# Pooled attention and a top-1 mixture of experts on one core: one PSUM ring, a shifted attention stream, a later gate chain, a reordered start and a column-split last block

## Chip, cores, metric

The kernel runs on one core of one Trainium2 chip (trn2). The metric is the device time of one execution in microseconds (us), as the median of repeated runs. Every profile below is of one execution.

## What is computed

Eight batches, eight heads, 576 tokens, head size 64. Keys and values are averaged over groups of 8 tokens, so each head has 72 keys. The attention output (4608 tokens of 512) goes through a cosine router that takes one of eight experts per token; the experts are two layers, 512 to 1024 to 512.

```python
k_p = k.reshape(B, H, Sp, pool, D).mean(axis=3)
v_p = v.reshape(B, H, Sp, pool, D).mean(axis=3)
attn = softmax(scale * np.matmul(q, k_p.transpose(0, 1, 3, 2)))
x = np.matmul(attn, v_p)            # then tokens x 512
logits = (x / |x|) @ (emb / |emb|).T / tau
expert_idx = np.argmax(logits, axis=1)
gate_w = softmax(logits)[expert_idx]
out[mask] = gate_w[mask] * (np.maximum(x[mask] @ w1[e], 0.0) @ w2[e])
```

## The kernel before

For each batch the kernel picks the expert that most of its tokens choose, loads that expert's weights and runs its FFN over all 576 tokens; tokens that chose another expert are put right in a loop at the end, which runs zero times when there are none.

`attn_steps(b)` lists the attention of a batch: pooling of k and v (`_pool`, L179: matmuls with a 0/1 matrix `pmat`, two 64-row halves in turn), transposes of q (`qtr`, L200, L206) and of pooled k (`_kpt`), eight score heads (L241) each with an exponential on ScalarE (L248), five chunks of 128 tokens of PV (L265) with the division on VectorE (reciprocal `r` L272, scaling `x_sb` L274), their transposes into `xt_all` (L285, L290), routing (L312) and the choice (`_expert`, L330 to L384). `_expert` counts tokens per expert, GpSimd reads the index and starts the two weight loads (L89, L92). Then comes the gate chain: GpSimd takes a power (`ssq`, L355), VectorE scales the logits (L357 to L364), ScalarE takes their exponential (L367), VectorE makes the gate `gm` (L369 to L378).

`ffn_steps` lists an FFN: 16 groups of the first layer (`hgrp`, 4 matmuls of 288 columns, L406), evicted in turn by ScalarE (L411) and VectorE (L413) into `hT`; then five blocks of output rows (`yblk`, 8 matmuls of 512 columns, L423), the fifth with 64 rows, scaled by the gate on VectorE (L434) or ScalarE (L431) and stored by the sync queue (SP).

Attention of batches 0 and 1 runs alone; then `merge` interleaves FFN b with the attention of b + 2, in proportion to a cost noted beside each step. FFN 6 and 7 run alone. The order written is the order on each engine. PSUM has 8 banks: two 2-bank tiles `pa` for attention and four 1-bank tiles `pf` for the FFN. GpSimd's queue carries the loads of k, v, q and the weights; each costs it time to write descriptors.

Of the kernel before, what the change touches and what calls it, by code (L numbers as in the profile page):

```python
# [2 lines left out]

# [9 lines left out]
I32 = mybir.dt.int32  # L13

# [12 lines left out]
def kernel(  # L27
# [25 lines left out]

    const = ctx.enter_context(tc.tile_pool(name="const", bufs=1))
# [12 lines left out]
    def psa():  # L67
        return ps_a.tile([128, 1024], FP32, name="pa")

    def psf():  # L70
        return ps_f.tile([128, 512], FP32, name="pf")


    def load_qkv(b):
        kv = inp.tile([128, 2, HP, T * D], FP16, name="kv")
        qq = inp.tile([128, HP, T * D], FP16, name="qq")

        def view(a):
            return a[b].rearrange("(hp h2) (p t) d -> (h2 p) hp (t d)", h2=2, t=T)

        nc.gpsimd.dma_start(out=kv[:, 0], in_=view(k))
        nc.gpsimd.dma_start(out=kv[:, 1], in_=view(v))
        nc.gpsimd.dma_start(out=qq, in_=view(q))
        return kv, qq
# [13 lines left out]
    loads = {0: load_qkv(0)}  # L98


    ident_h = const.tile([128, 128], FP16)
    make_identity(nc, ident_h)
    ident_f = const.tile([128, 128], FP32)
    make_identity(nc, ident_f)
    loads[1] = load_qkv(1)

    pmat = const.tile([128, T, G], FP16)
    nc.vector.memset(pmat, 1.0)
    for half in range(2):
        sl = pmat[ts(half, 64)]  # L110
        nc.gpsimd.affine_select(out=sl, in_=sl, pattern=[[1, T], [-POOL, G]],
                                compare_op=ALU.is_ge, fill=0.0, base=0,
                                channel_multiplier=T)
        nc.gpsimd.affine_select(out=sl, in_=sl, pattern=[[-1, T], [POOL, G]],
                                compare_op=ALU.is_ge, fill=0.0, base=POOL - 1,
                                channel_multiplier=-T)
    ones_m = const.tile([128, 128], FP16)
    nc.vector.memset(ones_m, 1.0)
    iota8 = const.tile([128, E], FP32)
    nc.gpsimd.iota(iota8, pattern=[[1, E]], base=0, channel_multiplier=0,  # L120
                   allow_small_or_imprecise_dtypes=True)
    tie = const.tile([128, E], FP32)
    nc.vector.tensor_scalar(out=tie, in0=iota8, scalar1=-1e-7 * XS, scalar2=None,
                            op0=ALU.mult)
    tie_n = const.tile([128, E], FP32)
    nc.vector.tensor_scalar(out=tie_n, in0=iota8, scalar1=-0.001, scalar2=None,
                            op0=ALU.mult)
    half_c = const.tile([128, NC], FP32)
    nc.vector.memset(half_c, 0.5)
    pair_b = const.tile([1, B * E], I32)  # L130
    nc.gpsimd.iota(pair_b, pattern=[[1, B], [0, E]], base=0, channel_multiplier=0)
    pair_e = const.tile([1, B * E], I32)
    nc.gpsimd.iota(pair_e, pattern=[[0, B], [1, E]], base=0, channel_multiplier=0)

    enT = const.tile([128, 4, E], FP16)
    emb = const.tile([E, DM], FP32)
    nc.sync.dma_start(out=emb, in_=moe_expert_emb)
    emb_sq = const.tile([E, DM], FP32)
    emb_n = const.tile([E, 1], FP32)
    nc.scalar.activation(out=emb_sq, in_=emb, func=AF.Square, accum_out=emb_n)  # L140
    nc.gpsimd.tensor_tensor(out=emb_n, in0=emb_n, in1=half_c[:E, 0:1], op=ALU.pow)
    nc.vector.tensor_scalar(out=emb_n, in0=emb_n, scalar1=1e-6, scalar2=tau,
                            op0=ALU.add, op1=ALU.mult)
    nc.vector.reciprocal(out=emb_n, in_=emb_n)
    nc.vector.tensor_scalar_mul(out=emb, in0=emb, scalar1=emb_n)
    ent_ps = psa()
    for w in range(4):
        nc.tensor.transpose(out=ent_ps[:, ts(w, E)], in_=emb[:, ts(w, 128)],
                            identity=ident_f[:E, :E])
    nc.vector.tensor_copy(out=enT, in_=ent_ps[:, 0:4 * E].rearrange("p (w e) -> p w e", e=E))  # L150
# [5 lines left out]
    ext_f = keep.tile([1, B, E], FP32)  # L156

    weights = {}
    gates = {}


    def attn_steps(b):
# [9 lines left out]
        @step(2.0)  # L172
        def _pool():
            kv, _ = loads[b]
            pk = psa()
            for t in range(T):
                for par in range(2):
                    rows = ts(par, 64)
                    nc.tensor.matmul(  # L179
                        out=pk[0:G, ts(par, 512)],  # L180
                        lhsT=pmat[rows, t, :],
                        rhs=kv[rows, :, :, ts(t, D)].rearrange("p a h d -> p (a h) d"),
                        start=(t == 0), stop=(t == T - 1))
# [68 lines left out]
        for h in range(H):  # L252
            step(0.2)(lambda h=h: score(h))

        st['ssq'] = None

        def pv(c):
            if c == 0:
                st['ssq'] = rt.tile([128, NC], FP32, name="ssq")
                nc.vector.memset(st['ssq'], 1.0)  # L260
                st['xs'] = {}
            L = 128 if c < 4 else 64
            px = psa()
            for h in range(H):
                nc.tensor.matmul(  # L265
                    out=px[0:L, h * 128:h * 128 + D + 1],
                    lhsT=st['at', h][:, c * 128:c * 128 + L],
                    rhs=st['vpx'][:, h // 2, h % 2, :],
                    start=True, stop=True)
            pxv = px[0:L].rearrange("p (h c) -> p h c", c=128)  # L270
            r = xp.tile([128, H], FP32, name="r")
            nc.vector.reciprocal(out=r[0:L], in_=pxv[:, :, D])  # L272
            x_sb = xp.tile([128, H, D], FP16, name="x_sb")
            nc.vector.tensor_tensor(  # L274
                out=x_sb[0:L], in0=pxv[:, :, 0:D],
                in1=r[0:L].unsqueeze(2).to_broadcast([L, H, D]), op=ALU.mult)
            st['xs'][c] = x_sb

        def xtr(c):
# [3 lines left out]
            pt = psa().bitcast(FP16)  # L283
# [7 lines left out]
            else:  # L291
# [3 lines left out]
            sq = xp.tile([128, H * D], FP16, name="sq")  # L295
            nc.scalar.activation(out=sq[0:L], in_=xf[0:L], func=AF.Square,  # L296
                                 accum_out=st['ssq'][0:L, c:c + 1])

        order = [('p', 0), ('p', 1), ('x', 0), ('p', 2), ('x', 1), ('p', 3),
                 ('x', 2), ('p', 4), ('x', 3), ('x', 4)]  # L300
        for kind, c in order:
            if kind == 'p':
                step(0.5)(lambda c=c: pv(c))
            else:
                step(0.3)(lambda c=c: xtr(c))

        @step(1.0)
        def _route():
            pl = psa()
            for c in range(NC):  # L310
                for w in range(4):
                    nc.tensor.matmul(out=pl[:, ts(c, E)],  # L312
                                     lhsT=xt_all[:, b, w, ts(c, 128)], rhs=enT[:, w, :],
                                     start=(w == 0), stop=(w == 3))
            lg = rt.tile([128, NC, E], FP32, name="lg")
            nc.vector.tensor_tensor(
                out=lg, in0=pl[:, 0:NC * E].rearrange("p (c e) -> p c e", e=E),
                in1=tie.unsqueeze(1).to_broadcast([128, NC, E]), op=ALU.add)
            lmax = rt.tile([128, NC], FP32, name="lmax")
            nc.vector.tensor_reduce(out=lmax, in_=lg, axis=AX.X, op=ALU.max)  # L320
            oh = oh_all[:, b]
            nc.vector.tensor_tensor(out=oh, in0=lg,
                                    in1=lmax.unsqueeze(2).to_broadcast([128, NC, E]),
                                    op=ALU.is_ge)
# [70 lines left out]
    def ffn_steps(xt, get_w, get_gm, finish):  # L395
# [166 lines left out]
```

## Time and profile before

| | us |
|---|---|
| median of 3 runs (lowest, highest) | 313.42 (313.03, 313.93) |
| the profiled execution, its own time | 315.35 |
| its span, first to last instruction | 313.8 |
| TensorE busy in it | 245.4 |

PE is TensorE's matmuls, PEld its weight loads, DVE VectorE, ACT ScalarE, POOL GpSimd, SP the sync engine. A row of a timeline gives the start, the busy time and, in brackets, how long the engine had been idle and what released it. The granted clock is a share of 2.4 GHz (0.50 is 1.2 GHz). Line numbers are those of the kernel before; the changed kernel has its own.

### The profile page before, as it was taken

How to read it: one execution, taken by the hardware profiler on the slowest of the kernel's cores; microseconds unless marked ns; L12 is line 12 of the kernel's file. 1: busy time of each engine (PE TensorE's matmuls, PEld its weight loads, DVE VectorE, ACT ScalarE, POOL GpSimd, SP SyncE). 2: the span in 40 equal slices, each digit the busy share in tenths (PEclk: the TensorE clock that was granted, in tenths of full speed). 3: DMA queues.
4: the chain of work that ended last, by engine and by line, in shares of the span. 5: the costliest groups of instructions: out<-in, count | busy, mean ns of one | idle time of the engine just before them, and what ended most of it. 6: DMA issues, size and time to landing. Idle time of an engine off the chain costs nothing.

```text
span 313.8 us, 5182 instructions
## 1 busy us (share of the span) xinstructions
PE 245.4 (78%) x1980; PEld 141.0 (45%) x1981; DVE 144.7 (46%) x445; ACT 108.2 (34%) x252; POOL 45.1 (14%) x65
## 2 busy tenths in 40 slices
PE   0376737689995999869995989599995999299990
PEld 0234423446453644545453645264553545164740
DVE  1135552745563637363664455363835456332410
ACT  2036117325431273126422344037412642121410
POOL 8400050060006000140006000410012000300000
PEclk9985565589998699979999899969997999789998
DMA  6980099669945994299747994399539414784142
GB/s 104 207 142 2 0 169 209 120 106 210 210 104 93 209 207 95 63 190 208 146 102 121 210 192 104 62 206 207 117 77 179 90 37 104 123 157 111 41 99 58
DMA packets 26924, 40.75 MB, mean 130 GB/s; under 512 B 1800, under 2 KB 14088, under 8 KB 26896
## 3 DMA queue, kind: packets, MB, share of 16 engines
q0 software_dynamic: 21120, 30.94, 56.3%
q1 hardware_dynamic: 5776, 9.46, 12.9%
q8 instruction: 16, 0.26, 0.3%
q14 instruction: 12, 0.10, 0.1%
HBM read 61.88 MB, written 9.44 MB: 227 GB/s over the span
## 4 chain that ended last, share of the span: by engine, by line
PE 60%; DVE 14%; ACT 9%; POOL 8%; issue 5%; POOLq 1%; DVEq 0%; ACTq 0%
PE pf L423 20%; PE pf L406 19%; ACT at L248 6%; DVE x_sb L274 4%; PE pa L265 4%; PE pa L241 4%; PE pa L206 3%; PE pa L179 3%; POOL ssq L355 3%; DVE y_sb L434 2%; PE pa L312 2%; POOL w L92 2%; PE pa L285 2%; DVE kpT L224 1%; ACT hT L411 1%
## 5 line engine op out<-in xcount | busy, mean ns | idle before, releaser
L406 PE MATMUL pf<-xt_all,w 128*128 128x288 f16 x512 | 84.5, 313 | 25.7 <-ACT hT L411 25.7
L423 PE MATMUL pf<-w,hT 128*128 128x512 f16 (+1 forms) x320 | 78.7, 380 | 0.0
L406 PEld LDWEIGHTS <-w 128*128 128x128 f16 x512 | 50.4, 106 | 48.6 <-issue 31.1
L248 ACT ACTIVATE at<-pa 72x576 f16<-72x576 f32 x64 | 38.4, 646 | 16.7 <-PE pa L241 16.6
L413 DVE TENSOR_SCALAR hT<-pf 128x288 f16<-128x288 f32 x64 | 27.9, 450 | 29.2 <-PE pf L406 29.0
L423 PEld LDWEIGHTS <-hT 128*128 128x128 f16 (+1 forms) x320 | 28.3, 100 | 25.8 <-issue 0.8
L411 ACT ACTIVATE hT<-pf 128x288 f16<-128x288 f32 x64 | 25.6, 408 | 41.0 <-PE pf L406 41.0
L89 POOL DMA_DIRECT2D w<-in_moe_w_dram x8 | 6.1, 760 | 224.2 <-PE pf L406 117.5
L296 ACT ACTIVATE sq<-x_sb 128x512 f16<-128x512 f16 (+1 forms) x40 | 24.9, 625 | 20.0 <-DVE x_sb L274 19.8
L274 DVE TENSOR_TENSOR x_sb<-pa,r 128x512 f16<-128x512 f32 (+1 forms) x40 | 27.6, 690 | 2.8 <-ACT sq L296 0.5
L434 DVE TENSOR_SCALAR y_sb<-pf,gm 128x512 f32<-128x512 f32 (+1 forms) x24 | 17.9, 746 | 20.7 <-PE pf L423 20.7
L265 PE MATMUL pa<-vpx,at 72*128 72x65 f16 (+1 forms) x320 | 20.2, 208 | 8.3 <-DVE x_sb L274 5.4
L241 PE MATMUL pa<-qT,kpT 64*72 64x256 f16 (+1 forms) x128 | 21.7, 332 | 5.4 <-ACT at L248 2.9
L367 ACT ACTIVATE lg<-lg 128x40 f32<-128x40 f32 x8 | 1.9, 236 | 68.0 <-DVE lg L364 68.0
L431 ACT ACTIVATE y_sb<-pf,gm 128x512 f32<-128x512 f32 x16 | 11.0, 687 | 36.1 <-PE pf L423 36.1
L265 PEld LDWEIGHTS <-at 72*128 72x128 f16 (+1 forms) x320 | 15.6, 108 | 17.2 <-DVE x_sb L274 9.1
L272 DVE RECIPROCAL r<-pa 128x8 f32<-128x8 f32 (+1 forms) x40 | 8.1, 203 | 30.7 <-PE pa L265 30.7
L179 PE MATMUL pa<-kv,pmat 64*72 64x512 f16 x144 | 22.1, 462 | 0.0
L206 PE MATMUL pa<-ident_h,qq 128*128 128x128 f16 x128 | 15.5, 257 | 5.0 <-DVE vpx L190 5.0
L285 PE MATMUL pa<-ident_h,x_sb 128*128 128x128 f16 (+1 forms) x160 | 16.7, 234 | 2.3 <-DVE x_sb L274 2.3
L207 DVE COPY qT<-pa 128x1152 f16<-128x1152 f16 x16 | 12.1, 756 | 12.7 <-PE pa L206 12.5
L241 PEld LDWEIGHTS <-kpT 64*72 64x72 f16 x128 | 7.9, 113 | 21.4 <-issue 16.4
(82 smaller groups left out, 178.2 us busy)
## 6 DMA issues: line engine op xcount, KB each, us to landing
w<-in_moe_w_dram POOLq DMA_DIRECT2D x16, 1024.0 KB, 10.0
out_dram<-y_sb SPq DMA_DIRECT2D x72, 128.0 KB, 2.4
kv<-in_k_dram POOLq DMA_DIRECT2D x8, 576.0 KB, 13.8
kv<-in_v_dram POOLq DMA_DIRECT2D x8, 576.0 KB, 15.9
qq<-in_q_dram POOLq DMA_DIRECT2D x8, 576.0 KB, 18.0
emb<-in_moe_expert_emb_dram SPq DMA_DIRECT2D x1, 16.0 KB
```

Of the source, the lines that this page charges most:

```text
L179: nc.tensor.matmul(out=pk[0:G, ts(par, 512)], lhsT=pmat[rows, t, :], rhs=kv[rows, :, :, ts(t, D)].rearrange("p a h d -> p (a h) d"), start ...
L206: nc.tensor.transpose(out=pq[:, ts(blk, 128)], in_=src, identity=ident_h)
L241: nc.tensor.matmul(out=pS[0:G, c0:c0 + nb * 64].rearrange("g (t p) -> g t p", p=64), lhsT=st['kpT'][rows, h if j == 0 else h ^ 1, :], rhs= ...
L248: nc.scalar.activation(out=at, in_=pS[0:G, c0:c0 + S], func=AF.Exp, scale=escale)
L265: nc.tensor.matmul(out=px[0:L, h * 128:h * 128 + D + 1], lhsT=st['at', h][:, c * 128:c * 128 + L], rhs=st['vpx'][:, h // 2, h % 2, :], sta ...
L274: nc.vector.tensor_tensor(out=x_sb[0:L], in0=pxv[:, :, 0:D], in1=r[0:L].unsqueeze(2).to_broadcast([L, H, D]), op=ALU.mult)
L296: nc.scalar.activation(out=sq[0:L], in_=xf[0:L], func=AF.Square, accum_out=st['ssq'][0:L, c:c + 1])
L406: nc.tensor.matmul(out=ph[:, 0:HALF], lhsT=w1v[:, kk, w // 2, w % 2, :], rhs=xt()[:, kk, ts(half, HALF)], start=(kk == 0), stop=(kk == 3))
L411: nc.scalar.activation(out=dst, in_=ph[:, 0:HALF], func=AF.Relu)
L413: nc.vector.tensor_scalar(out=dst, in0=ph[:, 0:HALF], scalar1=0.0, scalar2=None, op0=ALU.max)
L423: nc.tensor.matmul(out=py[0:L, :], lhsT=st['hT'][:, w // 2, w % 2, c * 128:c * 128 + L], rhs=w2[:, w // 2, w % 2, :], start=(w == 0), stop ...
L434: nc.vector.tensor_scalar(out=y_sb[0:L], in0=py[0:L, :], scalar1=g, scalar2=None, op0=ALU.mult)
```

## The change

- PSUM: one ring of four 2-bank tiles for everything. A first-layer group is now a whole 576-token row block (two runs of 288 columns, one per bank, one eviction: even ones ScalarE, odd ones VectorE). Two y blocks share one tile.
- Order: attention is one stream of steps, with positions in batches; before each FFN step all stream steps up to 1.7 batches ahead are issued. FFN 0 so begins after 0.7 of batch 1.
- The gate chain (`norm`, `prob`, `gate`) is taken out of the choice and put 1.1, 1.2 and 1.3 batches after that batch's start.
- Start: k first, q in two halves, v last; `pmat` and the identity made on VectorE from two iotas; nine matmuls on ones; batch 0 pools k and v apart, and its expert is chosen from its first chunk of tokens.
- Routing and choice: tie offsets and counts are added by matmuls; `max` and `max_index` find the expert.
- The fifth y block is computed as two column halves (64 columns of the array each), 16 matmuls of 256 columns, evicted by both engines; PV's fifth chunk is computed twice, into both partition halves.

```diff
-    ps_a = ctx.enter_context(tc.tile_pool(name="ps_a", bufs=2, space=bass.MemoryType.PSUM))
-    ps_f = ctx.enter_context(tc.tile_pool(name="ps_f", bufs=4, space=bass.MemoryType.PSUM))
+    ps = ctx.enter_context(tc.tile_pool(name="ps", bufs=4, space=bass.MemoryType.PSUM))
+
+    def psum():
+        return ps.tile([128, 1024], FP32, name="pa")
...
+                for rows in ([ds(0, 128)] if c < 4 else [ds(0, 64), ds(64, 64)]):
+                    L = 128 if c < 4 else 64
+                    nc.tensor.matmul(
+                        out=px[rows, h * 128:h * 128 + D + 1],
...
+            pl = psum()
+            nc.tensor.matmul(out=pl[:, 0:n * E], lhsT=ones_m[0:1, 0:128],
+                             rhs=tie_l[:, 0:n * E], start=True, stop=False)
...
+            mx = rt.tile([128, E], FP32, name="mx")
+            nc.vector.max(out=mx, in_=pc[:, 0:E])
+            ix = rt.tile([1, E], U32, name="ix")
+            nc.vector.max_index(out=ix, in_max=mx[0:1], in_values=pc[0:1, 0:E])
...
+            ph = psum()
+            for half in range(2):
+                for kk in range(4):
+                    nc.tensor.matmul(out=ph[:, half * 512:half * 512 + HALF],
...
+            if w % 2 == 0:
+                nc.scalar.activation(out=dst, in_=src, func=AF.Relu)
...
+            if part == 0 and c % 2 == 0:
+                st['y'] = psum()
+            py = st['y'][:, ts(c % 2, 512)]
...
+        def ylast():
+            w2 = get_w()[1]
+            py = psum()
+            DH = DM // 2
+            for w in range(8):
+                for r in range(2):
+                    nc.tensor.matmul(out=py[ts(r, 64), r * 512:r * 512 + DH],
+                                     lhsT=st['hT'][:, w // 2, w % 2, 512:S],
+                                     rhs=w2[:, w // 2, w % 2, ts(r, DH)],
+                                     start=(w == 0), stop=(w == 7))
...
+        warm = psum()
+        for i in range(9):
+            nc.tensor.matmul(out=warm[:, 0:512], lhsT=ones_m[:, 0:128], rhs=ones_m,
+                             start=True, stop=True)
...
+            for c, f in steps:
+                astream.append((b + done / total, f))
+                done += c
+            for i, f in enumerate(gate_steps(b)):
+                astream.append((b + 1 + 0.1 * (i + 1), f))
...
+                while j < len(astream) and astream[j][0] < b + done / total + LEAD:
+                    astream[j][1]()
+                    j += 1
+                f()
```

GpSimd's queue, where a batch's expert is known, in the kernel before (`ssq` is the gate chain's power, `w` a weight, `kv` and `qq` the next batch's k, v, q):

```order
L89 DMA w_703<-in_moe_w_dram 128x4x1024
L92 ISA
L92 DMA w_704<-in_moe_w_dram 128x4x1024
L355 TENSOR_TENSOR ssq<-ssq,half_c 128x5
L81 DMA kv<-in_k_dram 128x4x576
L82 DMA kv<-in_v_dram 128x4x576
L83 DMA qq<-in_q_dram 128x4x576
```

and in the changed one:

```order
L93 DMA w_1239<-in_moe_w_dram 128x4x1024
L96 ISA
L96 DMA w_1240<-in_moe_w_dram 128x4x1024
L86 DMA kv<-in_k_dram 128x4x576
L87 DMA kv<-in_v_dram 128x4x576
L88 DMA qq<-in_q_dram 128x4x576
L394 TENSOR_TENSOR ssq<-ssq,half_c 128x5
```

The power moved behind three loads. On VectorE, the operations after the index of the expert (`ei`) in the kernel before; `rn` waits for that power, and the first `hT` eviction of the next FFN is 15 rows after the index:

```order
L349 TENSOR_SCALAR ei_1141<-ei_f_1139 1x1
L357 TENSOR_SCALAR rn_1158<-ssq_935 128x5
L359 RECIPROCAL rn_1158<-rn_1158 128x5
L361 TENSOR_TENSOR lg_1110<-lg_1110,lmax_1112 128x40
L364 TENSOR_TENSOR lg_1110<-lg_1110,rn_1158 128x40
```

and after the index (`ix`) in the changed kernel:

```order
L318 MAX_INDEX ix_1225<-mx_1223,pa_1216 1x8
L319 TENSOR_SCALAR eb_all_91<-pa_1216,mx_1223 128x8
L328 TENSOR_SCALAR pos_all_92<-pa_1216 1x8
L164 MEMSET vpx_1270 72x8
L165 CAST vpx_1270<-pa_1248 72x8x64
L444 TENSOR_SCALAR hT_1080<-pa_1273 128x576
L198 COPY qT_1295<-pa_1294 128x1152
L444 TENSOR_SCALAR hT_1080<-pa_1307 128x576
L211 COPY kpT_1326<-pa_1317 128x576
L198 COPY qT_1329<-pa_1328 128x1152
L398 TENSOR_SCALAR rn_1341<-ssq_990 128x5
```

`rn` moved behind six evictions and copies. On TensorE, from one y block to the next in an FFN that runs alone, in the kernel before (the wait shown is for VectorE's eviction L413 of a first-layer tile):

```order
L423 MATMUL pf_3679<-w2_3399,hT_3582 128x512
L423 LDWEIGHTS hT_3582 [waits Activation_49]
L423 MATMUL pf_3679<-w2_3399,hT_3582 128x512
L423 LDWEIGHTS hT_3582
L423 MATMUL pf_3692<-w2_3399,hT_3582 128x512 [waits DVE_49]
```

and in the changed one (the last wait shown is for VectorE's eviction L463 of the first block, out of the other half of the same tile):

```order
L453 MATMUL pa_3645<-w2_3445,hT_3564 128x512
L453 LDWEIGHTS hT_3564 [waits DVE_49]
L453 MATMUL pa_3645<-w2_3445,hT_3564 128x512
L453 LDWEIGHTS hT_3564
L453 MATMUL pa_3645<-w2_3445,hT_3564 128x512 [waits DVE_49]
```

The second block now writes the tile that the first is read from.

## Rows read from the trace of the kernel before

**Rows 1.** The page, whole span: busy time and share; a group of part 5.
```profile
PE 245.4 (78%) x1980; PEld 141.0 (45%) x1981; DVE 144.7 (46%) x445; ACT 108.2 (34%) x252; POOL 45.1 (14%) x65
...
L274 DVE TENSOR_TENSOR x_sb<-pa,r 128x512 f16<-128x512 f32 (+1 forms) x40 | 27.6, 690 | 2.8 <-ACT sq L296 0.5
```

**Rows 2.** Who waited for whom, TensorE: us in total, times, longest.
```profile
PE pf L406 <- ACT hT L411: 25.7, 11, 5.6
```

**Rows 3.** Windows: length, busy by engine (instructions), granted clock, DMA share, GB/s.
```profile
69.58:101.15 31.57, 26.88 (x243) 15.52 (x243) 16.72 (x49) 11.97 (x29) 4.05 (x5) 0.98 0.82 155
...
135.97:169.85 33.88, 29.10 (x248) 16.73 (x248) 17.73 (x55) 13.03 (x32) 4.92 (x7) 0.95 0.81 150
...
238.40:272.36 33.96, 26.92 (x229) 15.90 (x229) 17.69 (x55) 13.05 (x32) 2.77 (x3) 0.92 0.50 98
...
289.58:306.38 16.80, 16.76 (x105) 10.11 (x104) 5.91 (x11) 4.66 (x10) 0.00 (x0) 1.00 0.32 75
```

**Rows 4.** Timeline, one period's start: start, us, engine, line, what [idle before <-releaser].
```profile
133.39 1.21 POOL L355 TENSOR_TENSOR ssq<-ssq,half_c 128x5 f32<-128x5 f32 x1
...
134.64 0.17 DVE L357 TENSOR_SCALAR rn<-ssq 128x5 f32<-128x5 f32 x1 [4.22 <-POOL ssq L355]
...
135.38 0.24 ACT L367 ACTIVATE lg<-lg 128x40 f32<-128x40 f32 x1 [8.57 <-DVE lg L364]
...
135.97 0.65 PE L406 MATMUL pf<-xt_all,w 128*128 128x288 f16 x4 [3.39 <-ACT hT L411]
```

**Rows 5.** Timeline, TensorE after that wait.
```profile
141.26 0.39 PE L206 MATMUL pa<-ident_h,qq 128*128 128x128 f16 x4
...
141.99 1.14 PE L406 MATMUL pf<-xt_all,w 128*128 128x288 f16 x8
```

**Rows 6.** Timeline, scores, pooling and choice of expert later in that period.
```profile
144.80 0.32 PE L241 MATMUL pa<-qT,kpT 64*72 64x320 f16 x2
...
145.05 0.67 PE L406 MATMUL pf<-xt_all,w 128*128 128x288 f16 x4
...
162.75 2.13 PE L179 MATMUL pa<-kv,pmat 64*72 64x512 f16 x18
...
164.16 0.14 DVE L349 TENSOR_SCALAR ei<-ei_f 1x1 int32<-1x1 f32 x1
...
165.79 0.74 POOL L89 DMA_DIRECT2D w<-in_moe_w_dram  x1 [28.95 <-PE pf L406]
```

**Rows 7.** Timeline, the prologue.
```profile
13.17 4.05 PE L179 MATMUL pa<-kv,pmat 64*72 64x512 f16 x18
...
21.36 4.78 ACT L248 ACTIVATE at<-pa 72x576 f16<-72x576 f32 x8 [3.25 <-PE pa L241]
...
38.53 0.80 POOL L89 DMA_DIRECT2D w<-in_moe_w_dram  x1 [26.93 <-issue]
...
47.57 4.78 ACT L248 ACTIVATE at<-pa 72x576 f16<-72x576 f32 x8 [4.51 <-PE pa L241]
```

**Rows 8.** Windows, a stretch of the prologue (columns as in 3).
```profile
48.00:56.00 8.00, 5.66 (x44) 2.94 (x43) 2.84 (x7) 5.72 (x12) 0.00 (x0) 0.50 1.18 209
```

**Rows 9.** Timeline, second layer of the last FFN, and the end.
```profile
297.43 8.91 PE L423 MATMUL pf<-w,hT 128*128 128x512 f16 x40
...
299.42 0.75 DVE L434 TENSOR_SCALAR y_sb<-pf,gm 128x512 f32<-128x512 f32 x1 [1.33 <-PE pf L423]
...
304.43 1.43 PEld L423 LDWEIGHTS <-hT 128*64 128x64 f16 x8 [0.42 <-issue]
304.54 0.69 ACT L431 ACTIVATE y_sb<-pf,gm 128x512 f32<-128x512 f32 x1 [2.72 <-PE pf L423]
306.38 0.74 DVE L434 TENSOR_SCALAR y_sb<-pf,gm 64x512 f32<-64x512 f32 x1 [2.76 <-PE pf L423]
```

**Rows 10.** Instructions by tile: transfers of k, v (prologue), then of the weights.
```profile
DMA to landing us min/median/max: 5.9/12.2/16.0
...
DMA to landing us min/median/max: 7.7/10.0/13.3
```

More of the change, by code (lines that the diff above doesn't have):

```diff
@@ L96, in load_w @@
         return w1, w2
[L98 to L116, printed above, removed]
@@ L128 @@
[L128 to L139, printed above, removed]
@@ L150 @@
-    nc.vector.tensor_copy(out=enT, in_=ent_ps[:, 0:4 * E].rearrange("p (w e) -> p w e", e=E))
+    weights = {}
+    gates = {}
+    routes = {}
     xt_all = keep.tile([128, B, 4, NC * 128], FP16)
@@ L307, in _route, with route @@
[L307 to L310, printed above, removed]
+            sq = xp.tile([128, H * D], FP16, name="sq", bufs=1)
+            nc.scalar.activation(out=sq, in_=xf, func=AF.Square,
+                                 accum_out=st['ssq'][:, c:c + 1])
+        def route(c0, n):
+            pl = psum()
+            nc.tensor.matmul(out=pl[:, 0:n * E], lhsT=ones_m[0:1, 0:128],
+                             rhs=tie_l[:, 0:n * E], start=True, stop=False)
+            for c in range(n):
@@ new lines, in route @@
+                                     lhsT=xt_all[:, b, w, ts(c0 + c, 128)],
+                                     rhs=enT[:, w, :],
+                                     start=False, stop=(c == n - 1 and w == 3))
+            plv = pl[:, 0:n * E].rearrange("p (c e) -> p c e", e=E)
+            if 'lg' not in st:
+                st['lg'] = rt.tile([128, NC, E], FP32, name="lg")
+                st['lmax'] = rt.tile([128, NC], FP32, name="lmax")
+            cs = ds(c0, n)
+            lmax = st['lmax'][:, cs]
@@ new lines, in route, with count @@
+            bc = lmax.unsqueeze(2).to_broadcast([128, n, E])
+            nc.vector.tensor_reduce(out=lmax, in_=plv, axis=AX.X, op=ALU.max)
+            nc.vector.tensor_tensor(out=oh_all[:, b, cs], in0=plv, in1=bc, op=ALU.is_ge)
+            nc.vector.tensor_tensor(out=st['lg'][:, cs], in0=plv, in1=bc, op=ALU.subtract)
+        def count(cs, pc):
+            nc.tensor.matmul(out=pc[:, 0:E], lhsT=ones_m[0:1, 0:128], rhs=tie_n,
+                             start=True, stop=False)
+            for c in cs:
+                nc.tensor.matmul(out=pc[:, 0:E], lhsT=ones_m[:, 0:128],
+                                 rhs=oh_all[:, b, c], start=False, stop=(c == cs[-1]))
@@ L352, in _expert, with present, recount, next_load @@
                                    max_val=E - 1)
             weights[b] = load_w(e_val)
+        def present(pc):
+            nc.vector.tensor_scalar(out=pos_all[:, b], in0=pc[0:1, 0:E], scalar1=0.5,
+                                    scalar2=None, op0=ALU.is_ge)
+        def recount():
+            pc = psum()
+            count(list(range(NC)), pc)
+            present(pc)
+        def next_load():
+            if b == 0:
+                load_qkv(2)
+            elif b + 2 < B:
+                load_qkv(b + 2)
@@ new lines, in attn_steps @@
+        if b == 0:
+            step(1.0)(pool_k)
+            step(0.5)(kpt)
+            step(0.8)(lambda: qtr(0))
+            for h in range(4):
+                step(0.65)(lambda h=h: score(h))
+            step(0.8)(lambda: qtr(1))
+            for h in range(4, 8):
+                step(0.65)(lambda h=h: score(h))
+            step(0.3)(emb_transposed)
+            step(1.0)(pool_v)
+        else:
+            step(2.0)(pool_kv)
+            step(0.8)(lambda: qtr(0))
+            step(0.5)(kpt)
+            step(0.8)(lambda: qtr(1))
+            for h in range(8):
+                step(0.65)(lambda h=h: score(h))
@@ new lines, in attn_steps @@
+        P = lambda c: step(0.9)(lambda: pv(c))
+        X = lambda c: step(0.6)(lambda: xtr(c))
+        P(0)
+        P(1)
+        X(0)
+        if b == 0:
+            step(0.4)(lambda: route(0, 1))
+            P(2)
+            step(0.4)(lambda: expert([0]))
+            step(0.0)(next_load)
+        else:
+            P(2)
+        X(1)
+        P(3)
+        X(2)
+        P(4)
+        X(3)
+        X(4)
+        if b == 0:
+            step(0.8)(lambda: route(1, 4))
+            step(0.4)(recount)
+        else:
+            step(1.0)(lambda: route(0, NC))
+            step(0.4)(lambda: expert(list(range(NC))))
+            if b >= 1:
+                step(0.0)(next_load)
@@ L451, in store @@
     def store(b):
         o_b = out[ts(b, S)]
-        def finish(c, L, y_sb):
-            for j in range(L // 64):
-                nc.sync.dma_start(out=out_rows(o_b, c, j), in_=y_sb[ts(j, 64)])
-        return finish
-    def run(steps):
-        for _, f in steps:
-            f()
-    def merge(a, bs):
-        ta = sum(c for c, _ in a) or 1.0
-        tb = sum(c for c, _ in bs) or 1.0
-        i = j = 0
-        ca = cb = 0.0
-        while i < len(a) or j < len(bs):
-            if j >= len(bs) or (i < len(a) and ca / ta <= cb / tb):
-                c, f = a[i]
-                i += 1
-                ca += c
-            else:
-                c, f = bs[j]
-                j += 1
-                cb += c
-            f()
@@ L480, with finish, emb_transposed @@
-    with tc.manual_schedule():
-        run(attn_steps(0))
-        run(attn_steps(1))
-        for b in range(B):
-            fs = ffn_steps(lambda b=b: xt_all[:, b], lambda b=b: weights[b],
-                           lambda b=b: gates[b], store(b))
-            merge(fs, attn_steps(b + 2) if b + 2 < B else [])
+        def finish(c, y_sb):
+            for dst, src in out_rows(o_b, c, y_sb):
+                nc.sync.dma_start(out=dst, in_=src)
+        return finish
+    def emb_transposed():
+        pe = psum().bitcast(FP16)
+        for w in range(4):
+            nc.tensor.transpose(out=pe[:, ts(w, E)], in_=emb_h[:, ts(w, 128)],
+                                identity=ident_h[:E, :E])
+        nc.vector.tensor_copy(out=enT, in_=pe[:, 0:4 * E].rearrange("p (w e) -> p w e", e=E))
```

374 lines of the change are left out of this document (199 added, 175 removed).

## The prediction

> **What bounds the kernel now.** I read the page's busy shares first, then who waited for whom, then windows cut at the starts of the FFNs, then the timeline of one such period, then the prologue. TensorE is busy for 78% of the span [rows 1] and no other engine passes 46%. Its one large wait is 25.7 us in 11 pieces, at the first layer's matmuls (L406) for ScalarE's eviction (L411) [rows 2]. The windows [rows 3] split the span of 313.8 us: 69.6 before the first FFN, six periods of one FFN merged with one attention (69.58 to 272.36, 33.8 each), two bare FFNs (17.2 and 16.8), and a tail of 7.4.
>
> In one period [rows 4] GpSimd does the power of the gate chain (1.21) only after both weights' descriptors. VectorE stands 4.22 at L357 for it; ScalarE, whose queue is in order, waits 8.57 with the chain's exponential, in front of the eviction L411; TensorE stands 3.39 with all four single-bank tiles full. Afterwards it runs slowly for some 5 us (clock 0.95 over the period [rows 3]). So each period loses the wait and then clock. In the prologue nothing overlaps: a chain of evictions, with TensorE at the lower level, 1.2 GHz (0.50) [rows 8].
>
> **The period, step by step.**
> - Gate chain. It now stands behind the next batch's copies on VectorE, while GpSimd's power moves behind three more descriptor writes (k, v, q). Power ready: some 0.9 from the count to the index, 1.5 from the index (164.16+0.14) to the first weight's issue at 165.79, five writes at 0.76, 1.2 of power: 7.4 after the count [rows 4, 6]. Before VectorE reaches the chain, TensorE must do 18 pooling matmuls (2.1), 24 of L435 (2.9), 20 transposes (1.5) and 8 small ones (0.3), and VectorE must copy the last transposes (about 0.75 and 0.2 to start): 7.8 [rows 5, 6, 9]. The margin is 0.4 without any wait of TensorE's; I take the wait as gone: -3.39.
> - Clock. 20 L406 matmuls and 10 transposes fill 135.97 to 141.26, 5.29 us [rows 4, 5]. In a bare FFN 64 such matmuls take 7.85 (289.58 to 297.43 [rows 3, 9]), so 20 take 2.45; the next ten transposes take 0.73 (141.26 to 141.99): -2.1, a wait of 0.40 in the stretch included.
> - Last y block. Eight 64-column matmuls of 512 become 16 of 256, two at a time in the two column halves. Evictions come 1.84 apart there, 1.71 for a full block [rows 9]. No row shows column halves at work together; the nearest, 64-row halves, do: 18 pooling matmuls of 512 columns take 2.13 [rows 6], 118 ns each, against 1.71/8 = 214. Bounds: 0.9, and 1.84 or more. I take 1.1 with the change of form: -0.75.
> - Tie and count as matmuls, six more per batch, of 8 or 40 columns: bounded by nothing and by the 118 ns above; I take 40 ns, +0.25. They shorten the chain to the weights, which has slack.
> - One ring. First-layer tiles are now evicted at 576 columns: ScalarE 0.60, by its exponentials of 576 [rows 7], VectorE about 0.84, by 0.75 at 512 [rows 9]; four each for eight each. That is beside TensorE's 0.98 for each, and costs nothing unless an engine is late.
> - **A new wait.** Two y blocks share one two-bank tile, and the order shows the second block's first matmul waiting for VectorE's eviction of the first. Between them stand only two score pairs (0.25 each: from 144.80 to 145.05 [rows 6]) or one PV group (about 0.3). The eviction starts 0.28 after the last matmul (297.43 + 1.71 to 299.42) and takes 0.75: 1.0 [rows 9]. Uncovered: at least 0.5 less what the block before it hides; I take 0.35 and 0.55: +0.9, with bounds 0 and 2.0.
> - The other waits, 33.88 - 29.10 - 3.39 - 0.40 = 1.0 [rows 3, 4], I carry over: less at PV, some at the routing, which needs VectorE's last copy of xt.
>
> 33.88 - 3.39 - 2.1 - 0.75 + 0.25 + 0.9 = 28.8. Six: 172.8, and 1 more because the first starts at the lower clock.
>
> **The start.** k lands 5.9 after an issue at about 1.5 [rows 10], at 7.4. The pooling matrix came from GpSimd, and TensorE pooled first at 13.17; now VectorE makes it from two iotas. Three operations on 648 elements (0.8 each, from 0.75 at 512) and five small ones of 0.2 or less after iotas at about 3 end at 6.4, under the landing; GpSimd's two iotas take 0.3 each at most by estimate and delay q, v by as much. The nine warm-up matmuls run before and cost nothing. Pooling of k alone: 18 matmuls of 256 columns, half of 4.05 [rows 7] or half of 2.13; 1.6: 9.0. Two copies, kpT, transposes, qT, all serial, some 3.6: first exponential at 12.6, against 21.36 [rows 7]. Eight take 4.8; the v pooling lies behind the scores (2.0), its copy 0.7: PV at 18.9. Five chunks at about 1.3 of VectorE (0.69 of it the scaling L274 [rows 1]) and ten small operations of the routing and choice: second count at 29.3. Then pooling of batch 1 at the lower clock 3.9, its copies (one on ScalarE, four on VectorE) 4.0, the gate chain 0.8: eight exponentials from 38.0 to 42.9, before from 47.57 [rows 7]. PV 0 to transposes 1 take 3.3: the first FFN starts at **46**, not 69.6, with 0.3 of batch 1 to do. Its weights are issued at about 26 instead of 38.53 [rows 7] and land by 37, so they are no bound.
>
> **The end.** FFN 7: first layer 7.85, four blocks 6.85, last 1.1, two uncovered half-tile waits of 1.0 [rows 9]: 17.8, for 16.8. FFN 6: the same and what is left of attention 7, some 3.4: 21.2. Tail: the last eviction is half as wide (0.74 to 0.45): 7.1 for 7.4 [rows 9]. Ten stores a batch instead of nine go through the sync queue, off the path.
>
> 46.0 + 172.8 + 1 + 21.2 + 17.8 + 7.1 = 265.9 of span. The profiled execution took 315.35 with 313.8 of span, and the median shown is 313.42: 265.9 + 1.55 = 267.5 for such a run, 1.9 less for the median, **265.5**.
>
> **Rivals.**
> 1. Column halves do not overlap. For it: no row shows that they do. The block stays at 1.84, +0.8 in each of eight: 272. Worse if their weight loads cannot hide: 16 loads of 0.18 (1.43/8) and 16 half-length matmuls of 0.107 one after another are 4.6, +3.5 each: 293. Against the worse: eight loads and eight matmuls of 64 columns fit in 1.84, so loads hide there [rows 9]. The Trainium skill, "TensorE: Matmul & The Clock Gate", Part 3, lets a weight load overlap running matmuls only where the row group differs. By that rule these 16 come out as in the 293, and the row speaks against it. Chance 0.2, of it 0.03 for the worse.
> 2. The chain stays late. The margin is 0.4; one late index uses it up. 1 to 3.4 in seven batches: 272 to 289. For: ScalarE still holds the exponential in front of the scores' evictions. 0.08.
> 3. Better than forecast. The warm-up leaves the higher level for the prologue (three poolings at half the time and other pieces: -4), and half-tile waits are hidden (-0.9 in six): 250 to 258. Against: after the warm-up TensorE idles some 2 us, and waits such as the prologue's went with 0.50 before [rows 8]. 0.17.
> 4. **Slower than before:** the weights come late. The choice of expert now stands 0.7 of a period ahead of the first use, not a whole one. From the issue to the first L435 of that batch I count 17.6; landing takes 7.7 to 13.3, median 10.0 [rows 10]. Each us beyond 17.6 is a us per period; to eat 48 us in seven batches landing must take 24.4. For it: a period moves 150 GB/s x 33.88 = 5.08 MB; in 28.8 that is 176 GB/s, and 209 is what a full stretch shows [rows 3, 8]. 0.03.
> 5. Stalls of the old size reappear in the shared ring, with every tile behind an eviction in order: no change, 0.02.
>
> **How the numbers follow.** Forecast 0.5, its own range 258 to 272; rivals 1 to 5 as given. The range 250 to 280 leaves out rivals 4 and 5, the worse part of 1, half of 2 and a little below 250. A measurement tells 0.3% (1 us) from no change. Faster 0.95 (the first four cases), same 0.02, slower 0.03.
>
> **What would show it.** Right: no wait of L435 for ScalarE over 1 us; first L435 near 46; periods near 28.8 at a clock near 1.0; L453 waiting for y_sb (L463), about 1.0 twice in the last FFN. The 16 matmuls of the last block start 55 to 65 ns apart on average if halves overlap, 107 if not. Wrong: VectorE's L398 waiting over 1 us for the power; L435 waiting for a weight's transfer; a first L435 after 50.

## The result and the profile after

The changed kernel takes **260.34 us** (median of four runs, 259.59 to 260.54), the kernel before 313.23 beside it: a ratio of 0.8305, 95% interval 0.8282 to 0.8327. The profiled execution took 260.54 with 258.6 of span.

The page of the changed kernel, busy time and two groups of part 5, for [rows 1, 2]:

```profile
PE 224.4 (87%) x2186; PEld 140.0 (54%) x2187; DVE 131.1 (51%) x371; ACT 109.3 (42%) x227; POOL 42.2 (16%) x59
...
L453 PE MATMUL pa<-w,hT 128*128 128x512 f16 x256 | 64.3, 379 | 9.5 <-DVE y_sb L463 9.5
L435 PE MATMUL pa<-xt_all,w 128*128 128x288 f16 x512 | 72.2, 290 | 0.0
```

L435 is the first layer, before L406: its 25.7 us of waiting for ScalarE are gone, and a new wait of 9.5 at the second layer is the largest that TensorE has. The windows of the changed kernel (columns as in [rows 3]), cut at the first L435 of each FFN and at the last matmul's end; of five equal periods one is shown:

```profile
0.00:45.49 45.49, 31.32 (x285) 19.93 (x287) 21.12 (x69) 17.32 (x37) 11.78 (x23) 0.66 0.88 151
45.49:74.40 28.91, 27.61 (x272) 17.02 (x271) 15.95 (x45) 12.56 (x27) 4.98 (x6) 0.94 0.74 137
...
129.16:156.53 27.37, 26.07 (x272) 16.19 (x270) 15.56 (x44) 13.42 (x28) 4.97 (x6) 1.00 0.97 188
...
211.28:232.49 21.21, 18.79 (x178) 11.99 (x176) 10.77 (x36) 7.44 (x16) 2.74 (x3) 1.00 0.59 113
232.49:250.53 18.04, 16.24 (x114) 10.10 (x112) 5.01 (x7) 4.45 (x7) 0.00 (x0) 1.00 0.47 116
250.53:258.60 8.07, 0.00 (x1) 0.00 (x0) 0.47 (x1) 0.47 (x1) 0.00 (x0) 0.68 0.24 54
```

The windows of the kernel before in [rows 3] cannot be set beside these as they are: they are cut where the first layer goes on after its wait for ScalarE, and not where an FFN starts. Its FFN 0 starts at 61.58, not at 69.58, and its FFN 6 at 264.63, 7.7 us ahead of the cut at 272.36:

```profile
61.58 1.13 PE L406 MATMUL pf<-xt_all,w 128*128 128x288 f16 x4
...
264.63 2.12 PE L406 MATMUL pf<-xt_all,w 128*128 128x288 f16 x16
272.36 8.54 PE L406 MATMUL pf<-xt_all,w 128*128 128x288 f16 x48 [5.61 <-ACT hT L411]
```

With both kernels cut at first matmuls, the first FFN starts 16.1 us earlier; the six merged periods take 165.8 for 203.1; FFN 6, which now holds the rest of attention 7, still takes 3.7 less, with its wait of 5.61 gone; FFN 7 takes 1.2 more and the end 0.7 more. That is -16.1 - 37.3 - 3.7 + 1.2 + 0.7 = -55.2, the difference of the two spans. The length of a middle period, 33.88, is the same with either cut.

The timeline of one merged period of the changed kernel, for [rows 4, 6]:

```profile
138.98 0.80 POOL L93 DMA_DIRECT2D w<-in_moe_w_dram  x1 [22.17 <-issue]
...
142.72 1.24 POOL L394 TENSOR_TENSOR ssq<-ssq,half_c 128x5 f32<-128x5 f32 x1
144.77 0.16 DVE L398 TENSOR_SCALAR rn<-ssq 128x5 f32<-128x5 f32 x1
...
145.43 0.33 ACT L405 ACTIVATE lg<-lg,lnxs 128x40 f32<-128x40 f32 x1 [3.42 <-DVE lg L402]
...
146.95 1.02 PE L453 MATMUL pa<-w,hT 128*128 128x512 f16 x4 [0.48 <-DVE y_sb L463]
...
152.74 1.02 PE L453 MATMUL pa<-w,hT 128*128 128x512 f16 x4 [0.47 <-DVE y_sb L463]
...
155.30 1.06 PE L473 MATMUL pa<-w,hT 128*64 128x256 f16 x16
156.30 0.40 PE L268 MATMUL pa<-ident_h,x_sb 128*128 128x128 f16 x4
```

GpSimd's power is ready at 143.96, VectorE asks for it at 144.77. ScalarE still waits 3.42 in front of the chain's exponential, but no first-layer eviction is queued there now. TensorE waits twice at a y block (0.48 and 0.47) and once, 0.35, at the routing.

The prologue of the changed kernel, for [rows 7]:

```profile
1.62 3.42 PE L534 MATMUL pa<-ones_m 128*128 128x512 f16 x9 [1.62 <-DVE half_c L522]
7.33 1.80 PE L145 MATMUL pa<-kv,pmat 64*72 64x256 f16 x18 [2.28 <-DVE emb_h L573]
13.39 2.26 ACT L235 ACTIVATE at<-pa 72x576 f16<-72x576 f32 x4 [3.64 <-PE pa L228]
20.96 1.06 PE L248 MATMUL pa<-vpx,at 72*128 72x65 f16 x16 [0.78 <-DVE vpx L165]
27.33 0.76 POOL L93 DMA_DIRECT2D w<-in_moe_w_dram  x1 [19.17 <-DVE x_sb L257]
30.35 4.05 PE L145 MATMUL pa<-kv,pmat 64*72 64x512 f16 x18
38.52 4.39 ACT L235 ACTIVATE at<-pa 72x576 f16<-72x576 f32 x8
```

### The profile page after: what moved, and what is told of

Same layout as the page of the kernel before. It is cut to its first block, busy times and chain, and to the rows that moved or that the text cites. A ratio compares the mean times of both kernels' runs of the same rounds, so it can differ in the third digit from the quotient of the medians.

```text
span 258.6 us, 5504 instructions
## 1 busy us (share of the span) xinstructions
PE 224.4 (87%) x2186; PEld 140.0 (54%) x2187; DVE 131.1 (51%) x371; ACT 109.3 (42%) x227; POOL 42.2 (16%) x59
## 5 line engine op out<-in xcount | busy, mean ns | idle before, releaser
L453 PE MATMUL pa<-w,hT 128*128 128x512 f16 x256 | 64.3, 379 | 9.5 <-DVE y_sb L463 9.5
L435 PE MATMUL pa<-xt_all,w 128*128 128x288 f16 x512 | 72.2, 290 | 0.0
L435 PEld LDWEIGHTS <-w 128*128 128x128 f16 x512 | 47.7, 99 | 13.8 <-issue 2.6
L453 PEld LDWEIGHTS <-hT 128*128 128x128 f16 x256 | 22.3, 97 | 35.1 <-issue 15.2
L442 ACT ACTIVATE hT<-pa 128x576 f16<-128x576 f32 x32 | 20.8, 651 | 35.9 <-PE pa L435 35.6
L463 DVE TENSOR_SCALAR y_sb<-pa,gm 128x512 f32<-128x512 f32 x16 | 12.0, 751 | 38.8 <-PE pa L453 38.8
L444 DVE TENSOR_SCALAR hT<-pa 128x576 f16<-128x576 f32 x32 | 24.1, 754 | 11.5 <-PE pa L435 11.5
L257 DVE TENSOR_TENSOR x_sb<-pa,r 128x512 f16<-128x512 f32 x40 | 27.7, 692 | 2.5
L279 ACT ACTIVATE sq<-x_sb 128x512 f16<-128x512 f16 x40 | 25.0, 625 | 8.4 <-DVE x_sb L257 6.5
L461 ACT ACTIVATE y_sb<-pa,gm 128x512 f32<-128x512 f32 x16 | 11.0, 687 | 32.2 <-PE pa L453 32.2
L145 PE MATMUL pa<-kv,pmat 64*72 64x512 f16 (+1 forms) x162 | 20.8, 409 | 2.5 <-DVE emb_h L573 2.3
L268 PE MATMUL pa<-ident_h,x_sb 128*128 128x128 f16 (+1 forms) x160 | 16.1, 228 | 2.3 <-DVE x_sb L257 2.3
## 6 DMA issues: line engine op xcount, KB each, us to landing
w<-in_moe_w_dram POOLq DMA_DIRECT2D x16, 1024.0 KB, 10.7
```

The lines of the kernel that those rows point to most:

```text
L145: nc.tensor.matmul(out=pk[0:G, par * 512 + c0:par * 512 + c0 + na * HP * D], lhsT=pmat[rows, t, :], rhs=kv[rows, a0:a0 + na, :, ts(t, D)]. ...
L257: nc.vector.tensor_tensor(out=x_sb, in0=pxv[:, :, 0:D], in1=r.unsqueeze(2).to_broadcast([128, H, D]), op=ALU.mult)
L268: nc.tensor.transpose(out=pt[:, w * 128:w * 128 + L], in_=xf[0:L, ts(w, 128)], identity=ident_h[:L, :L])
L279: nc.scalar.activation(out=sq, in_=xf, func=AF.Square, accum_out=st['ssq'][:, c:c + 1])
L435: nc.tensor.matmul(out=ph[:, half * 512:half * 512 + HALF], lhsT=w1v[:, kk, w // 2, w % 2, :], rhs=xt()[:, kk, ts(half, HALF)], start=(kk ...
L442: nc.scalar.activation(out=dst, in_=src, func=AF.Relu)
```

## The experiments

Ratios are to the kernel before, run on the same chip; the changed kernel's own is 0.8305. The times of stages are from the profiles.

### The gate chain, put back and moved alone

The chain directly behind the choice of expert again:

```diff
-                astream.append((b + 1 + 0.1 * (i + 1), f))
+                astream.append((b + 0.9999, f))
```

> The changed kernel with the gate chain of a batch put back directly behind its choice of expert, ahead of the next batch's loads and pooling. Theory: the chain's place is the cause of the old wait; ScalarE again stands in its queue in front of the first layer's evictions, and a merged period loses 3.4 of wait and up to 2.1 of clock: period 30 to 33, time 280 to 298. Rival: the ring's two-bank tiles (twice the first-layer work ahead of an eviction, and shared) cover the stall, and the deferral was needed for at most 1 us a period: 260 to 268.

Measured: 284.86 us, ratio 0.9041 (0.9012 to 0.907); four of the five middle periods 31.0 to 31.1, one 29.5. Its timeline in one period:

```profile
119.77 1.21 POOL L394 TENSOR_TENSOR ssq<-ssq,half_c 128x5 f32<-128x5 f32 x1
121.02 0.17 DVE L398 TENSOR_SCALAR rn<-ssq 128x5 f32<-128x5 f32 x1 [3.88 <-POOL ssq L394]
121.68 0.33 ACT L405 ACTIVATE lg<-lg,lnxs 128x40 f32<-128x40 f32 x1 [5.03 <-DVE lg L402]
...
123.35 0.88 PE L435 MATMUL pa<-xt_all,w 128*128 128x288 f16 x3 [2.20 <-ACT hT L442]
```

The old wait is back, 2.2 where it was 3.39 [rows 4]; that the shared ring's larger tiles cover the difference is my reading, and no run tests them alone. Those four periods are 3.6 to 3.8 longer than the changed kernel's: some 2.2 of wait, and the rest is work done slower behind it, for their granted clock is 0.94 or 0.95. The one of 29.5 has a wait of 1.98 and a clock of 1.00.

The other way round, the kernel before with the deferral alone (the chain, unchanged, becomes a function that the next batch calls):

```diff
+            def gate():
-            nc.gpsimd.tensor_tensor(out=st['ssq'], ...)
+                nc.gpsimd.tensor_tensor(out=st['ssq'], ...)
...
+            pending.append(gate)
...
+        if b > 0:
+            step(0.0)(lambda: pending.pop(0)())
```

> The kernel before with one part of the change alone: the gate chain of a batch (power, softmax, gates) goes behind the next batch's transposed keys, in front of its scores, and for the last batch into FFN 6. Theory: the wait of L406 for L411 goes (3.4 in each period) and the clock lost after it (2.1): period 28.4 instead of 33.9, time 280 to 285. Rival: with four one-bank tiles the first layer still stalls behind some other eviction, so that less than half is won: 297 or more.

Measured: 278.56 us, ratio 0.8888 (0.8828 to 0.8948), 1.4 us under the theory's range. No wait of L413, there the first layer, for ScalarE is left, and a period takes 28.78. Alone in the kernel before, moving the chain wins 0.111, against 0.170 for the whole change; taken out of the changed kernel it costs 0.074. So it is the largest single part that was tested, and the parts do not simply add up.

### The last y block

Eight full-width matmuls again (with one eviction and one store):

```diff
-                for r in range(2):
-                    nc.tensor.matmul(out=py[ts(r, 64), r * 512:r * 512 + DH],
+                nc.tensor.matmul(out=py[0:64, 0:DM],
...
```

> The changed kernel with its last y block as before: eight matmuls of 512 columns into 64 rows, one eviction on VectorE, one store. Theory: column halves run at the same time, so the block costs eight times 0.214, 1.71, where the sixteen take 0.99; +0.72 in each of eight batches, period 28.1, time about 266 (265 to 268). Rival: the sixteen gain nothing that the period keeps, the time stays at 260 to 261.

Measured: 266.23 us, ratio 0.846 (0.8446 to 0.8474), as the theory had it. TensorE's timeline there: the eight take 1.85, the sixteen 1.00 (155.30 to 156.30 above); the period is 28.22, +0.85.

```profile
101.72 1.91 PE L471 MATMUL pa<-w,hT 128*64 128x512 f16 x8
103.57 0.40 PE L268 MATMUL pa<-ident_h,x_sb 128*128 128x128 f16 x4
```

Both halves kept, but one after the other:

```diff
-            for w in range(8):
-                for r in range(2):
+            for r in range(2):
+                for w in range(8):
```

> The changed kernel with the sixteen matmuls of the last y block in another order: all eight of the first column half, then all eight of the second. Theory: the gain is two column halves running at the same time, which needs matmuls of different halves next to each other; sixteen of 0.107 are then 1.71 instead of 0.99, period 28.1, time about 266 (265 to 267.5). Rival: the gain comes from 256 columns at a time or from the weight loads, whatever the order: 260 to 261.

Measured: 263.01 us, ratio 0.8359 (0.8337 to 0.838), between the two. The period is 27.84, and the block 1.46:

```profile
100.96 1.53 PE L473 MATMUL pa<-w,hT 128*64 128x256 f16 x16
102.42 0.40 PE L268 MATMUL pa<-ident_h,x_sb 128*128 128x128 f16 x4
```

So the order of the halves is worth 0.46 of the 0.85: alternate halves do run together (a start every 62 ns). The other 0.4 is overlap as well, as the starts in this trace show. They form two series of eight, which I take for the two halves, with 109 ns from start to start in each, close to the 107 of the theory; but the second series begins at 101.42, when three matmuls of the first are still to start. The theory was wrong in that halves written one after the other also run one after the other.

### The y blocks' tiles

```diff
-            if part == 0 and c % 2 == 0:
+            if part == 0:
                 st['y'] = psum()
-            py = st['y'][:, ts(c % 2, 512)]
+            py = st['y'][:, 0:512]
```

> The changed kernel with each y block of the second layer in a two-bank tile of its own. Theory: the sixteen waits of L453 for VectorE's eviction (9.5 us in all, 0.95 in each merged period) come only from two blocks sharing a tile; they go and nothing takes their place, period 26.4 instead of 27.38, time about 251 (249.5 to 252.5). Rival: each batch now takes two more tiles of the ring of four, so TensorE waits instead for an eviction three or four tiles back, at a score or PV group; period 27.0 or more, time 256 to 260.

Measured: 252.25 us, ratio 0.8031 (0.8011 to 0.8052): better than the change. The time lies in the theory's range, the period, 26.75, between theory and rival. Waits of TensorE:

```profile
PE pa L453 <- DVE y_sb L463: 2.4, 5, 0.5
...
PE pa L435 <- ACT y_sb L481: 1.2, 1, 1.2
```

One of the period's two waits is left, now at a tile four back in the ring. FFN 6 won most, 2.4, and FFN 7 won 0.7, though its first layer now waits 1.2 once for the eviction of the last y block before it.

### The lead

```diff
-    LEAD = 1.7
+    LEAD = 2.0
```

> The changed kernel with a lead of 2.0 batches instead of 1.7: all of batch 1's attention stands before the first FFN. Theory: the last 0.3 of batch 1 (PV 2 to the choice) then runs alone at the pace of batch 0's, some 6 us, and takes only 3.4 out of FFN 6: first L435 at 51 to 52 instead of 45.5, FFN 6 at 18.0 instead of 21.2, time 262 to 265. Rival: TensorE has the same work either way and the lead is worth nothing: 259 to 261.

Measured: 263.67 us, ratio 0.8404 (0.8366 to 0.8441); first L435 at 49.49, FFN 6 at 17.8. A lead of 1.7 is worth some 3 us against 2.0.

> The changed kernel with a lead of 1.5: the first FFN starts right behind batch 1's scores. Theory: first L435 at about 41, 4.3 us earlier, and some 2.2 us more work in FFN 6; the weights, chosen 0.58 of a period (15.9 us) before their first use, still land in time; time 257 to 259.5. Rival: the weights come late, L435 waits for their transfer in most periods, time 261 to 268.

Measured: 253.94 us, ratio 0.8083 (0.8042 to 0.8123), better than expected. First L435 at 41.54. What I had not foreseen is the period, 26.70: the transposes of q now lie between y blocks and hide one of the two waits. In the last FFN L435 waits 1.9 for its weights.

### The clock in the prologue

Twenty warm-up matmuls for nine, and then also matmuls that nobody reads where TensorE waited for operands (one such place shown):

```diff
-        for i in range(9):
+        for i in range(20):
```

```diff
+    def fill(tile_, n):
+        for _ in range(n):
+            nc.tensor.matmul(out=tile_[:, 0:512], lhsT=ones_m[:, 0:128], rhs=ones_m,
+                             start=True, stop=True)
...
             pS = psum()
+            fill(pS, 4 if b == 0 and h in (0, 4) else 2 if b == 1 and h == 0 else 0)
```

> The changed kernel with 20 warm-up matmuls instead of 9, and nothing else added. Theory: they only bridge the wait for k, so the pooling of k runs at the higher level (18 matmuls in 1.17 as with all the added ones), and the waits behind it bring the lower level back before the first score; first L435 at 44 to 46, time 259 to 261. Rival: the bridge alone keeps the higher level through the prologue, first L435 at 41 to 42, time 255 to 257.

> The changed kernel with matmuls added whose output nobody reads: 20 warm-up matmuls instead of 9, and two to four before batch 0's transposes of keys, scores 0 and 4, PV 0, transposes of x and routing, where TensorE waited for operands, and two before batch 1's first score. Theory: the prologue runs at the lower clock because TensorE idles; kept busy it stays at the higher level, pooling of k takes 0.95, batch 1's pooling 2.1, first L435 at 40 to 42 instead of 45.5, time 254 to 258. Rival: the added matmuls stand in the path or the level stays at 0.50: 261 to 266.

Measured: 258.86 us, ratio 0.8239 (0.8202 to 0.8276), with the bridge alone, and 256.02 us, ratio 0.8151 (0.8113 to 0.819), with all of them. TensorE's timeline with the bridge alone, and then with all:

```profile
1.62 7.45 PE L534 MATMUL pa<-ones_m 128*128 128x512 f16 x20 [1.62 <-DVE half_c L522]
9.01 1.17 PE L145 MATMUL pa<-kv,pmat 64*72 64x256 f16 x18
...
18.18 2.14 PE L145 MATMUL pa<-kv,pmat 64*72 64x256 f16 x18 [0.26 <-DVE vpx L164]
...
30.49 4.05 PE L145 MATMUL pa<-kv,pmat 64*72 64x512 f16 x18
```

```profile
8.21 1.17 PE L150 MATMUL pa<-kv,pmat 64*72 64x256 f16 x18
...
16.81 1.17 PE L150 MATMUL pa<-kv,pmat 64*72 64x256 f16 x18 [0.27 <-DVE vpx L169]
...
28.13 2.13 PE L150 MATMUL pa<-kv,pmat 64*72 64x512 f16 x18
...
41.35 2.13 PE L447 MATMUL pa<-xt_all,w 128*128 128x288 f16 x8
```

With the bridge alone the pooling of v and of batch 1 is back at the lower level's pace (2.14, 4.05), and the first L435 comes at 45.63, where it was; the 1.5 us between the medians does not show in this profile, which is of the slowest of its six runs and has a span of 258.6 too, and stays open. Kept busy in its waits too, TensorE pools everything in half the time and reaches the first FFN 4.1 us earlier, though the twenty, longer than the wait for k, push its pooling back by 0.9. The first L435 is at the lower pace again (eight in 2.13, for 1.14 later): nothing was added behind batch 1's first score.

### Together

> The changed kernel with three edits together: a tile of its own for each y block, the added matmuls of the prologue, and a lead of 1.5. Theory: the three act at different places, except that own tiles and the shorter lead both remove half-tile waits (9.5 us in all, counted once): 260.3 - 8.1 (own tiles) - 4.3 (added matmuls) - 2.3 (the rest of the lead) = 245.6, 244 to 248; period 26.1 to 26.5; the last FFN still waits some 2 us for its weights. Rival: they share more than that (the shorter lead gains only where the added matmuls already do, the weights come late more often): 249 to 252.

Measured: 250.62 us, ratio 0.799 (0.7957 to 0.8023): the rival's number. The period is 26.69: with the shorter lead the own tiles bring it nothing (26.70 with the lead alone), for a score now waits 0.58 for an eviction of y. The last FFN stands at its weights; a row of TensorE's waits:

```profile
PE pa L447 <- DMA w<-in_moe_w_dram: 4.3, 1, 4.3
```

> The same three edits with a lead of 1.6. Theory: first L435 some 1.5 us later than at 1.5, but the weights of every batch land before their first use, the last too: 244 to 247. Rival: the interleaving at 1.6 meets evictions at worse places: 248 to 251.

Measured: **247.03 us**, ratio 0.7878 (0.7836 to 0.792), period 26.46, no wait for an eviction of y in it; the last FFN waits 0.8 for its weights. It beats both kernels.

With the last block's end split (the second half's eviction into a tile of its own, its store from ScalarE's queue):

```diff
+            y_b = y_sb if rows8 is None else yp.tile([128, DM], FP32, name="y_sb")
...
+                nc.sync.dma_start(out=rows8[:, 0:DH], in_=y_sb[0:64, 0:DH])
+                nc.scalar.dma_start(out=rows8[:, DH:DM], in_=y_b[64:128, 0:DH])
```

> The three edits with a lead of 1.6, and in the last FFN the last y block's two halves in tiles of their own, the second half stored from ScalarE's queue. Theory: ScalarE's eviction stands behind VectorE's only because both write one tile, and the two stores behind each other on one queue: the end, from the last matmul's end to the end of the span 8.1 before, becomes 7.0 to 7.3, time 246 (245 to 246.8). Rival: the end is the landing of the last store and does not move: 247.

Measured: 246.56 us, ratio 0.7858 (0.7831 to 0.7885), not to be told from 0.7878. The end is 7.5 for 8.3 in the profiles, but that shows no gain: with the halves in sequence, two evictions and two stores as in the changed kernel, it took 7.25, and in the changed kernel 8.07. The stores go out side by side, but ScalarE's eviction still starts behind VectorE's:

```profile
236.20 0.48 DVE L491 TENSOR_SCALAR y_sb<-pa,gm 64x256 f32<-64x256 f32 x1 [1.92 <-PE pa L485]
236.76 0.47 ACT L494 ACTIVATE y_sb<-pa,gm 64x256 f32<-64x256 f32 x1 [0.82 <-DVE y_sb L491]
```

So the tile in SBUF was not the cause. The two still read one PSUM tile; giving them one each was not tried.

## Why the prediction was right, and where it was off

The forecast was 265.5, 5 us above the result, in the main for the reasons named; its sum of the span, 265.9, is 7.3 above 258.6. That the time came nearer than the span is luck: I took 1.9 off because the old profiled run lay that far above its median, and the changed kernel's lies 0.2 above.

- **The start** (46.0): 45.49. First exponential 13.39 for 12.6, PV 20.96 for 18.9, weights at 27.33 for 26. Links that were up to 2.1 late were made up behind it: batch 1's exponentials end at 42.91, as worked out (42.9), which owes something to luck, and the first FFN follows in 2.6, not 3.3. The 69.6 that I set beside the 46 is not the old FFN 0's start, which is 61.58: the start won 16.1 us. Of its parts only the lead and the warm-up were varied in runs; the rest of its worth is read from the two timelines.
- **The period** (28.8): 27.38, five times -1.42; the first, 28.91 for 29.8. This step carries the error. Three terms held: the gate wait went whole (the margin was 0.8, not 0.4), the clock came back, and the half-tile waits are 0.48 and 0.47 for 0.35 and 0.55. Mis-sized was what I carried over: other waits of 1.0 became 0.35, one at the routing, as the windows tell (27.37 - 26.07 is 1.30, of which 0.95 are half-tile waits). TensorE's busy time fell by 3.0 (29.10 to 26.07), where I had 2.2. The clock's part of it was sized right: a period of the kernel before with the deferral alone is busy for 27.30 at a clock of 1.00, 1.8 less, where 1.7 was in the sum (2.1 with a wait of 0.4):

```profile
117.45:146.24 28.79, 27.30 (x250) 16.05 (x250) 17.60 (x54) 13.25 (x31) 4.99 (x6) 1.00 0.91 176
```

The other changes took off 1.2, where I had 0.5. Groups of the same 64, 16 and 16 matmuls, of before and then of the changed kernel:

```profile
L406 PE MATMUL pf<-xt_all,w 128*128 128x288 f16 x64 | 10.8, 309 | 3.8 <-ACT hT L411 3.8
L241 PE MATMUL pa<-qT,kpT 64*72 64x320 f16 (+1 forms) x16 | 2.5, 306 | 0.2 <-ACT at L248 0.2
...
L206 PE MATMUL pa<-ident_h,qq 128*128 128x128 f16 x16 | 2.0, 265 | 0.0
```

```profile
L435 PE MATMUL pa<-xt_all,w 128*128 128x288 f16 x64 | 9.0, 286 | 0.0
...
L228 PE MATMUL pa<-qT,kpT 64*72 64x320 f16 (+1 forms) x16 | 2.0, 300 | 0.0
L197 PE MATMUL pa<-ident_h,qq 128*128 128x128 f16 x16 | 1.6, 220 | 0.0
```

The first layer gained 1.8 and the transposes of q 0.4, together more than the clock: in five places a score pair stood behind a first-layer matmul, which then held TensorE for 0.23 us to the next start instead of 0.12, and those pairs now stand between y blocks. The scores gained 0.5 at an unchanged time each: where two pairs stand next to each other, the second now starts 0.14 behind the first, before 0.25 or more. I had a term for neither. The last y block gave 0.85 for 0.75.

- **FFN 6 and 7** (21.2, 17.8): 21.21 and 18.04. The waits there are 0.84 to 1.22, where I had 1.0 twice. The 17.2 that I read for the old FFN 6 leaves out its first 16 matmuls and its wait: it took 24.95.
- **The end** (7.1): 8.07. I let two half-wide evictions run beside each other; ScalarE's waits for VectorE's, and the two end 1.03 behind the last matmul, where 0.45 was in the sum:

```profile
251.09 0.47 ACT L481 ACTIVATE y_sb<-pa,gm 64x256 f32<-64x256 f32 x1 [0.77 <-DVE y_sb L479]
```

The other 0.4 lies behind the evictions and stays open: with the halves in sequence the same end took 7.25.

- **Rival 1** did not come: the sixteen matmuls start 62 ns apart, and the plain block shows that it could have cost 0.85 a batch. The worse case, by the rule of the Trainium skill ("TensorE: Matmul & The Clock Gate", Part 3) that a weight load overlaps running matmuls only where the row group differs, did not come either, and the trace does not agree with that rule: sixteen loads of 0.11 and sixteen matmuls over all 128 rows fit in 1.00.
- **Rival 2**: with the chain in its old place the time, 284.9, lies in the range given (272 to 289); in the new place VectorE waited for the power once, 0.8, for batch 7 in FFN 6.
- **Rival 3** did not come: the half-tile waits stayed, and the warm-up's level is lost while k is pooled (1.80, between 1.17 and 2.13). What it would be worth if kept, 4, is what the added matmuls won (4.3).
- **Rival 4** did not come at a lead of 1.7: in the timeline above 17.55 us lie between issue and first L435 (156.53), landing takes 7.7 to 14.5 (median 10.7). At 1.5 L435 did wait for weights, once, 1.9 in the last FFN, and the kernel was still faster.
- **Rival 5** did not come: no L435 waits for an eviction by ScalarE.

## What to carry to other kernels

Look at what stands in an in-order queue in front of an eviction: moving one chain of small operations behind the next batch's work, with no work removed, won 0.111 by itself where the whole change won 0.170. When two blocks share a tile by halves, as here, the second waits for the eviction of the first, so count the work between one half's last matmul and the other's first against the eviction. After such a change ask of every wait that went what it had hidden, and of the start whether idle gaps cost the clock. And cut the windows of two kernels at the same instruction before you subtract them.

## What the runs showed of the hardware beyond that

The granted clock in the first microseconds is not what it seems. With a lead of 1.5 the window reads 1.00, while the eighteen pooling matmuls take 2.13, the lower level's pace (the bridge alone took 2.14 for the same pooling of v, in a window that reads 0.50, and the added matmuls 1.17):

```profile
6.00:12.00 6.00, 3.92 (x36) 3.16 (x36) 1.99 (x7) 0.58 (x1) 2.16 (x5) 1.00 1.21 207
```

```profile
7.19 2.13 PE L145 MATMUL pa<-kv,pmat 64*72 64x256 f16 x18 [1.55 <-DMA kv<-in_k_dram]
```

That trace has no record of the clock before 34.88, and where there is none the view reads 1.00. The nine warm-ups take 4.02 there, all at one pace; in the changed kernel's profile 3.42, the last at twice the pace, and k's pooling 1.80. The same nine instructions raised the level in some executions and not in others: of the seven traces with nine, k's pooling took 1.17 to 1.80 in five and 2.13 or 2.14 in two. So compare such prologues by the time of equal matmuls and not by their mean clocks, and read nothing into a difference of 1 us between the starts of two profiles: in the changed kernel and four of its variants with the same start, the first L435 came between 44.54 and 45.54.
